# Softmax row sums: from tile additions in SBUF to TensorE products with a column of ones, accumulated in PSUM beside the output

## The chip, the cores and the metric

The program runs on one core of one Trainium2 chip. The metric is the time of one execution on the device, in microseconds (us). A core has five engines that run their own instruction lists in order and wait for one another through semaphores: TensorE (PE, matrix products, written to PSUM), VectorE (DVE), ScalarE (ACT), GpSimd (POOL) and SyncE (SP), which here issues the transfers. "PEld" in the profile is TensorE loading the stationary operand of a product.

## The reference

The program computes an attention with a cluster mask and then a mixture of experts. The change is in the attention alone: for each of 4 x 8 heads, 768 queries and 768 keys of 64 numbers.

```python
mask = q_assign[:, :, :, None] == k_assign[:, :, None, :]      # 16 clusters, by argmax
scores = np.where(mask, scale * np.matmul(q, k.transpose(0, 1, 3, 2)), -1e9)
attn = np.exp(scores - np.max(scores, axis=-1, keepdims=True))
attn = attn / (np.sum(attn, axis=-1, keepdims=True) + 1e-09)    # the row sum
attn_out = np.matmul(attn, v)
# then: gates by softmax over all logits, 8 rounds of normalisation, 8 experts
# out += P[:, e:e+1] * (np.maximum(x @ w1[e], 0.0) @ w2[e])
```

The row sum is over keys. It is needed once for each query and head, and the kernel divides by it after the product with v.

## The kernel before, in words

**Layout.** Two heads make a pair; there are 16 pairs. The 768 queries and keys are cut into six tiles of 128 (NT = 6). Weights are held transposed: a tile `pe` has 128 keys on the partitions and queries in the free dimension. So a sum over keys is a sum over the partitions of six tiles.

**Chunks.** A head's weights come in nine chunks (`CHUNKS`). For each u of three there is key tile 2u against queries 0 to 511, key tile 2u+1 against queries 0 to 511, and both key tiles against queries 512 to 767. Each chunk is 512 columns wide.

**Stages of a pair.** The loaded q and k are transposed on PE (L557), copied, and split into a high and a low part (L571 to L575, where the low part is a subtraction on DVE or POOL). Each position is assigned to a cluster (`assign_pair`, L593 to L635). `max_chunk` (L697, L701) takes the largest score of every query on PE and DVE. `max_rows` (L714 to L733) turns these into rows of the operand by way of DVE, ACT, POOL and PE. `exp_chunk` forms the scores again (L765, L766) into one of two PSUM tiles, and ACT writes their exponentials to `pe` (L772); 14 such tiles exist (`PB`).

**Sums before.** At the end of `exp_chunk` the six key tiles of a head are added element by element in SBUF into a tile `psum` (L791), each addition on POOL or on DVE. `norm` then sums over the partitions: a product with ones (L861), a copy (L868), three transposes (L872), the addition of 1e-9 and of flags for rows with nothing to attend to (L875), and a reciprocal (L886). The result is cut into three bf16 pieces (L890, L893), transposed (L897), spread over the rows of both heads (L908), and multiplied into `xT` (L913).

**Output.** `values` runs once for a pair. For each u it waits until the six chunks of both heads exist, and issues eight products with v into `av` (L824; the heads take columns 0 to 63 and 64 to 127 of the array). After the third u comes a small correcting product (L832), and ACT copies `av` to `xT` (L844). There is one `av` in PSUM.

**What sets the order.** A planner in the program places the steps on the engines ahead of time. Each step has a key (urgency), a cost that is written in the code, and sometimes a choice of engines with a reluctance. The planned order of each engine is then fixed. After the attention come the gates and the experts, whose instructions are written out by hand; their first weights are prepared within the last stretch of the attention (L1127, L1128, L1143, L1144).

Of the kernel before, what the change touches and what calls it, by code (L numbers as in the profile page):

```python
# [8 lines left out]
F32 = mybir.dt.float32  # L9
# [5 lines left out]
ALU = mybir.AluOpType  # L15
# [4 lines left out]
BIG = float(2.0**100)  # L20
P = 128
# [135 lines left out]
def attn_moe_kernel(  # L157
# [11 lines left out]
    nc = tc.nc  # L169
# [10 lines left out]
    NA, NB = 3, 4  # L180
    PB = 14
    N0 = 512
# [26 lines left out]
    Q = 32  # L209
# [102 lines left out]
    with ExitStack() as actx:  # L312
# [10 lines left out]
        def misc_tile():  # L323
            return ps_x.tile([P, 512], F32, name="misc_ps")
# [73 lines left out]
        for x in range(2):  # L398
# [8 lines left out]
        nc.vector.tensor_tensor(out=three12, in0=three12, in1=ident[0 : 3 * R, 2 * R : 3 * R], op=ALU.add)  # L407
        spread = sm.tile([3 * R, NT, 2, D], BF16, name="spread", bufs=1)
        nc.vector.tensor_copy(
            spread, three12.rearrange("r (x i) -> r i x", x=2).unsqueeze(3).broadcast_to([3 * R, NT, 2, D])  # L410
        )

        free = iter([(last[nm, i], f"{nm}{i}") for nm, i in kept])
# [9 lines left out]
        COSTS = [0.66, 0.46, 0.432, 0.214, 0.42]  # L423
        RELUCT = [0.05, 0.05, 0.5, 0.1, 0.2, 0.05, 0, 0, 0.3]

# [41 lines left out]
        t_nat, t_sc, t_pe, t_nh, t_vn = Tokens(2), Tokens(1), Tokens(PB), Tokens(6), Tokens(2)  # L467
        t_sum = Tokens(4)

# [17 lines left out]
        def load_group(n):  # L487
# [15 lines left out]
            for i in range(1, NT):  # L503
                e = yield (POOL, 0.687, RELUCT[3]), (DVE, 0.33)
                if i == 1:
                    vsum = nat.tile([P, G, D], F32, name="vsum", bufs=1)
                (nc.gpsimd if e == POOL else nc.vector).tensor_tensor(  # L507
                    out=vsum, in0=vn[:, :, 0, :] if i == 1 else vsum, in1=vn[:, :, i, :], op=ALU.add
                )
# [68 lines left out]
        def assign_pair(p):  # L578
# [128 lines left out]
        def max_rows(n):  # L707
# [12 lines left out]
            if n >= 8:  # L720
                yield ev["norm", n // 2 - 4]
            yield POOL, 0.1
            o = n % 2 * NT
            nc.gpsimd.tensor_scalar(out=flags[n // 2 % 4][:, o : o + NT], in0=mr, scalar1=-BIG / 2, scalar2=None, op0=ALU.is_le)
            yield t_x
# [22 lines left out]
        def exp_chunk(n, c):  # L748
# [26 lines left out]

            if c == 0:
                yield t_sum
                t["sum"] = work.tile([P, S], F32, name="psum", bufs=4)
                t["add"] = {}
            st, old = t["sum"], t["add"]  # L780
            if ni == 1:
                parts = [pe[:, 0]]
            else:
                parts = [pe[:, 0], pe[:, 1]]
            for part in parts:
                if a not in old:
                    old[a] = part
                    continue
                n_ = z - a
                e = yield (POOL, 0.33 + n_ * 0.0019), (DVE, 0.1 + n_ * 0.00125, RELUCT[2])  # L790
                (nc.gpsimd if e == POOL else nc.vector).tensor_tensor(out=st[:, a:z], in0=old[a], in1=part, op=ALU.add)  # L791
                old[a] = st[:, a:z]
            ev["s", n, c].set(plan)

        def release(p, c):

            c2 = c + 1 if c == 0 else c
            for x in range(2):
                yield ev["s", 2 * p + x, c2]
                t_pe.put(plan)  # L800

        def values(p):
# [10 lines left out]
            for u in range(NCH // 3):  # L813
# [36 lines left out]
        def norm(p):  # L850

            n = 2 * p
            b, h = divmod(n, H)
            for x in range(2):
                yield ev["s", n + x, NCH - 1]
            yield t_x
            yield PE, 0.75, 0.107, 0.64
            HS = S // 2
            ps = misc_tile()
            for g in range(4):  # L860
                nc.tensor.matmul(  # L861
                    ps[g * Q : (g + 1) * Q, 0:HS], ones[:, 0:Q], heads[n + g // 2]["sum"][:, g % 2 * HS : (g % 2 + 1) * HS], start=True, stop=True
                )
            for x in range(2):
                t_sum.put(plan)
            yield ACT, 0.48
            sc = work.tile([P, HS], F32, name="sc")
            nc.scalar.copy(sc, ps[:, 0:HS])  # L868
            yield PE, 0.36, 0.107, 0.1
            ps2 = misc_tile()  # L870
            for j in range(NT // 2):
                nc.tensor.transpose(out=ps2[:, j * P : (j + 1) * P], in_=sc[:, j * P : (j + 1) * P], identity=ident)  # L872
            yield DVE, 0.2
            rs = work.tile([P, R], F32, name="rs")
            nc.vector.scalar_tensor_tensor(  # L875
                out=rs.rearrange("p (g j) -> p g j", g=4),
                in0=ps2[:, 0 : NT // 2 * P].rearrange("p (j g q) -> p g j q", g=4, q=Q)[:, :, :, 0],
                scalar=1e-9,
                in1=flags[p % 4].rearrange("p (g j) -> p g j", g=4),
                op0=ALU.add,  # L880
# [546 lines left out]
```

## Time and profile before

| what | value |
|---|---|
| median of 3 runs | 2445.54 us (2442.27 to 2445.68) |
| the profiled execution, from its first to its last instruction | 2448.7 us, 3.2 above that median |
| mean granted TensorE clock | 0.984 |
| PE, DVE, ACT, POOL busy | 97%, 55%, 34%, 27% of the span |
| end of the attention's last output product | about 519 us |
| first product of the experts (L1219) starts | 532.4 us |
| L791, additions of weight tiles | 270 on POOL, 50 on DVE |

A group of instructions in the profile shows the line, the engine, the tiles written and read, the shapes (partitions x elements), the count, the busy time and mean duration, and the idle time of the engine just before them. A PE instruction's busy time includes its tail in the array, which overlaps with the next one's start. What a product holds the array for is therefore read from the distance of the starts, as the chain of waits lists it. A product of 32-bit floats appears as two instructions, and the page counts both; instruction lists of the program count it once. PEclk is the granted clock as a share of full speed.

### The profile page before, as it was taken

To read this page: it belongs to the slowest core of one execution; us is meant where nothing else is said; L and a number is where in the kernel's file an instruction comes from. 1 tells how busy PE (TensorE), PEld (TensorE's weight loads), DVE (VectorE), ACT (ScalarE), POOL (GpSimd) and SP (SyncE) were. 2 spreads that over 40 slices of the span, in tenths; PEclk is the share of its full clock that TensorE was granted. 3 is DMA by queue.
4 is the path that set the end of the run, shared out by engine and by line. 5 is a ranking of instruction groups with operands and counts; after the bars stand their busy time and mean duration, and the time that the engine had idled before them with its cause. 6 is when DMAs were issued, how large, how long until landed. Compare 5 with 4: busy or idle time off the path is not lost.

```text
span 2448.7 us, 32683 instructions
## 1 busy us (share of the span) xinstructions
PE 2383.3 (97%) x12848; PEld 1275.6 (52%) x12848; DVE 1342.4 (55%) x2354; ACT 836.1 (34%) x1616; POOL 672.4 (27%) x712
## 2 busy tenths in 40 slices
PE   7999999978999999999999999999999999999999
PEld 4555556534545555555555554555555555555554
DVE  7888888867655454545454445544444434444444
ACT  4555566544343333333333322212122121222211
POOL 5776777654153322223333201000000000000000
PEclk7999999989999999999999999999999999999999
DMA  6545465334466353535443334232222322223222
GB/s 145 119 101 121 102 150 152 84 125 155 164 220 218 146 196 133 212 142 186 171 156 129 127 135 145 95 113 99 95 95 96 111 102 95 95 95 109 104 104 90
DMA packets 154681, 320.29 MB, mean 131 GB/s; under 512 B 61088, under 2 KB 90528, under 8 KB 154016
## 3 DMA queue, kind: packets, MB, share of 16 engines
q1 hardware_dynamic: 154528, 318.21, 39.4%
q8 instruction: 101, 1.65, 0.3%
q14 instruction: 52, 0.43, 0.1%
HBM read 230.74 MB, written 58.72 MB: 118 GB/s over the span
## 4 chain that ended last, share of the span: by engine, by line
PE 86%; DVE 7%; issue 3%; ACT 2%; DMA 1%; POOL 0%; SPq 0%; POOLq 0%; ACTq 0%; DVEq 0%
PE h_ps L1219 34%; PE o_ps L1289 13%; PE o_ps L1287 13%; PE o_ps L1288 13%; PE av_ps L824 4%; PE max_ps L697 3%; PE exp_ps L765 2%; DVE mrt L701 2%; PE exp_ps L766 2%; DVE vsum L507 1%; PE misc_ps L557 1%; DVE hl L1235 1%; PE misc_ps L861 0%; ACT pe L772 0%; PE misc_ps L940 0%
## 5 line engine op out<-in xcount | busy, mean ns | idle before, releaser
L1219 PEld LDWEIGHTS <-wa 128*128 128x128 f16 x5376 | 528.1, 98 | 451.7 <-issue 26.9
L1219 PE MATMUL h_ps<-xsT,wa 128*128 128x384 f16 x3072 | 585.1, 327 | 9.2 <-DVE csum L1055 7.8
L1289 PE MATMUL o_ps<-wb,hl 128*128 128x512 f16 x1536 | 583.2, 380 | 1.4 <-DVE hl L1235 1.4
L1232 ACT ACTIVATE hh<-c 128x384 f16<-128x384 f32 x512 | 267.5, 523 | 927.7 <-DVE c L1247 916.6
L1288 PE MATMUL o_ps<-wb,hh 128*128 128x512 f16 x1536 | 583.1, 380 | 0.0
L1287 PE MATMUL o_ps<-wb,hh 128*128 128x512 f16 x1536 | 583.0, 380 | 0.0
L1235 DVE SCALAR_TENSOR_TENSOR hl<-c,hh 128x384 f16<-128x384 f32 x512 | 291.0, 568 | 493.1 <-ACT hh L1232 492.6
L1219 PE MATMUL h_ps<-xsB,wa 128*128 128x384 f16 x2304 | 421.4, 328 | 7.4 <-DVE c L1247 7.4
L1247 DVE SCALAR_TENSOR_TENSOR c<-h_ps,u 128x384 f32<-128x384 f32 x256 | 142.2, 555 | 193.1 <-PE h_ps L1219 193.0
L1289 PEld LDWEIGHTS <-hl 128*128 128x128 f16 x1536 | 150.5, 98 | 184.6 <-DVE hl L1235 3.4
L1247 DVE SCALAR_TENSOR_TENSOR u<-h_ps,m 128x384 f32<-128x384 f32 x256 | 142.3, 556 | 182.6 <-PE h_ps L1219 182.5
L791 POOL TENSOR_TENSOR psum<-psum,pe 128x512 f32<-128x512 f32 (+1 forms) x207 | 227.2, 1115 | 54.2 <-ACT pe L772 46.6
L1287 PEld LDWEIGHTS <-hh 128*128 128x128 f16 x1536 | 151.0, 98 | 139.2 <-issue 0.6
L1288 PEld LDWEIGHTS <-hh 128*128 128x128 f16 x1536 | 150.4, 98 | 139.6 <-issue 0.6
L701 DVE TENSOR_REDUCE mrt<-max_ps 128x1 f32<-128x512 f32 (+1 forms) x288 | 190.5, 683 | 46.3 <-PE max_ps L697 44.6
L1252 ACT ACTIVATE c<-h_ps 128x384 f32<-128x384 f32 x128 | 62.7, 490 | 424.7 <-PE h_ps L1219 424.7
L772 ACT ACTIVATE pe<-exp_ps 128x512 f32<-128x512 f32 x288 | 166.5, 597 | 88.8 <-PE exp_ps L766 82.6
L1101 POOL TENSOR_TENSOR r<-r 128x256 f32<-128x256 f32 x124 | 88.3, 733 | 372.4 <-ACT r L1092 370.0
L1307 DVE SCALAR_TENSOR_TENSOR acc<-o_ps,gates,acc 128x512 f32<-128x512 f32 x168 | 125.4, 747 | 41.3 <-PE o_ps L1289 41.1
L824 PE MATMUL av_ps<-pe,vn 128*64 128x512 f32 (+1 forms) x768 | 138.5, 504 | 0.0
L697 PE MATMUL max_ps<-kX,qX 96*128 96x256 f32 (+1 forms) x384 | 126.9, 393 | 5.5 <-DVE mrt L701 2.6
L766 PE MATMUL exp_ps<-qX,kX 98*128 98x512 f32 (+1 forms) x384 | 128.5, 347 | 0.0
(200 smaller groups left out, 1920.8 us busy)
## 6 DMA issues: line engine op xcount, KB each, us to landing
wa<-wd SPq DMA_DIRECT2D x96, 896.0 KB
wb<-wd SPq DMA_DIRECT2D x96, 512.0 KB
r<-in_moe_w SPq DMA_DIRECT2D x64, 512.0 KB
wd<-wa SPq DMA_DIRECT2D x32, 896.0 KB
scan<-in_moe_w SPq DMA_DIRECT2D x56, 512.0 KB
wd<-wb SPq DMA_DIRECT2D x32, 512.0 KB
qn<-in_q SPq DMA_DIRECT2D x16, 384.0 KB
kn<-in_k SPq DMA_DIRECT2D x16, 384.0 KB
```

The costliest lines, as they stand in the source:

```text
L697: nc.tensor.matmul(ps[:, y * (z - a) : (y + 1) * (z - a)], t["qa"][0:96, i * P : (i + 1) * P], t["k2"][0:96, a:z], start=True, stop=True)
L701: nc.vector.tensor_reduce(out=t["mr"][:, i0 : i0 + ni, ni - 1], in_=ps.rearrange("p (x c) -> p x c", x=ni), axis=AX, op=ALU.max)
L766: nc.tensor.matmul(o, t["k2"][0:98, ki], t["qa"][0:98, a:z], start=False, stop=True)
L791: (nc.gpsimd if e == POOL else nc.vector).tensor_tensor(out=st[:, a:z], in0=old[a], in1=part, op=ALU.add)
L824: nc.tensor.matmul(av[o, a:z], vn[:, i, :], heads[t]["pe", c][:, i - i0], start=(i == 0), stop=False, skip_group_check=True)
L1219: nc.tensor.matmul(ps[:, 0:HB], wa[:, w_, a, c, :], x[:, x_, c, :], start=(first and s_ == 0), stop=(s_ == len(steps) - 1), skip_group_che ...
L1232: nc.scalar.activation(hh[:, 2 - i, o], src, AF.Relu)
L1235: nc.vector.scalar_tensor_tensor(out=hl[:, 2 - i, o], in0=src, scalar=0.0, in1=hh[:, 2 - i, o], op0=ALU.max, op1=ALU.subtract)
L1247: nc.vector.scalar_tensor_tensor(out=t, in0=ps[:, 0:HB], scalar=KAPPA, in1=x, op0=ALU.mult, op1=ALU.add)
L1287: nc.tensor.matmul(po[i], hh[:, t, ti], wbh[:, t], start=(first and t == 0), stop=False)
L1288: nc.tensor.matmul(po[i], hh[:, t, ti], wbl[:, t], start=False, stop=False)
L1289: nc.tensor.matmul(po[i], hl[:, t, ti], wbh[:, t], start=False, stop=(last and t == 1))
```

## The change

The additions at the end of `exp_chunk` go, and with them the tiles `psum` and the process `release` that freed a weight tile once it was added and used. In their place, `values` issues after its eight output products of each u another 24: stationary is `pick`, 128 x 32, all zero but for a column of ones, moving are 128 queries of a weight tile, and the result goes to columns 768 to 895 of `av`, in the same bank of PSUM as the last 256 output columns. A block of 32 rows there belongs to one of four column blocks of the array. `piece` says which: query tiles 0 to 3 go to blocks 0 to 3, with one row for each head, and tiles 4 and 5 of both heads share the four blocks in a third row. So row sums accumulate over all key tiles in PSUM. After the last u ACT copies the 128 columns (`sc`), one transpose replaces three, and the rest of `norm` is as before, with `flags` and `spread` in the new order.

With it come: 20 weight tiles (`PB`), all six of a u given back after its 24 products; flags written by two POOL instructions and not one; and other reluctances, by which the planner gives the value sums (`vsum`), a product of the assignment (`ix`) and the low parts (`qL`, `kL`) to POOL where it can.

```diff
-    PB = 14
+    PB = 20
...
+        QG = P // Q
+        assert NT == QG + 2
...
+        pick = sm.tile([P, 3, Q], F32, name="pick", bufs=1)
+        nc.vector.memset(pick, 0.0)
+        for s_ in range(3):
+            nc.vector.memset(pick[:, s_, s_ : s_ + 1], 1.0)
+
+        def piece(x, i):
+            return (i, x) if i < QG else (2 * x + i - QG, 2)
...
-        RELUCT = [0.05, 0.05, 0.5, 0.1, 0.2, 0.05, 0, 0, 0.3]
+        RELUCT = [0.05, 0.05, 0.5, 0.1, 0.2, 0.05, 0.5, 0, 0.3]
...
-                e = yield (POOL, 0.687, RELUCT[3]), (DVE, 0.33)
+                e = yield (POOL, 0.687), (DVE, 0.33, RELUCT[2])
...
-            e = yield (DVE, 0.469), (POOL, 0.86, RELUCT[8])
+            e = yield (DVE, 0.469, RELUCT[8]), (POOL, 0.86)
...
-            for part in parts:
-                if a not in old:
-                    old[a] = part
-                    continue
-                n_ = z - a
-                e = yield (POOL, 0.33 + n_ * 0.0019), (DVE, 0.1 + n_ * 0.00125, RELUCT[2])
-                (nc.gpsimd if e == POOL else nc.vector).tensor_tensor(out=st[:, a:z], in0=old[a], in1=part, op=ALU.add)
-                old[a] = st[:, a:z]
-            ev["s", n, c].set(plan)
...
-                    plan.spawn(release(p, c), plan.now.key)
+                yield PE, 1.32, 0.107, 0.1
+                for k_ in (2 * u, 2 * u + 1):
+                    for i0, i1 in ((0, QG), (QG, NT)):
+                        for x in range(2):
+                            c = 3 * u + (k_ % 2 if i0 == 0 else 2)
+                            pe = heads[n + x]["pe", c][:, k_ - CHUNKS[c][0]]
+                            for i in range(i0, i1):
+                                g, s_ = piece(x, i)
+                                nc.tensor.matmul(
+                                    av[g * Q : (g + 1) * Q, S : S + P],
+                                    pick[:, s_],
+                                    pe[:, (i - i0) * P : (i - i0 + 1) * P],
+                                    start=False,
+                                    stop=(k_ == NT - 1 and s_ == 2),
+                                    skip_group_check=True,
+                                )
+                for _ in range(6):
+                    t_pe.put(plan)
+            yield ACT, 0.3
+            sc = heads[n]["sc"] = work.tile([P, P], F32, name="sc")
+            nc.scalar.copy(sc, av[:, S : S + P])
+            ev["sums", p].set(plan)
...
-            yield PE, 0.75, 0.107, 0.64
-            HS = S // 2
-            ps = misc_tile()
-            for g in range(4):
-                nc.tensor.matmul(
-                    ps[g * Q : (g + 1) * Q, 0:HS], ones[:, 0:Q], heads[n + g // 2]["sum"][:, g % 2 * HS : (g % 2 + 1) * HS], start=True, stop=True
-                )
...
-            for j in range(NT // 2):
-                nc.tensor.transpose(out=ps2[:, j * P : (j + 1) * P], in_=sc[:, j * P : (j + 1) * P], identity=ident)
+            nc.tensor.transpose(out=ps2[:, 0:P], in_=heads[n]["sc"], identity=ident)
```

Line numbers shift: the eight output products are at L824 before and L811 after, the 24 new ones at L822, the correcting product at L832 and L840, the copy of the sums at L868 and L834.

Three places show how instructions move. The first is PE at the end of the second pair's third u, with what each row waits for. Before:

```order
L697 MATMUL max_ps<-kX_156,qX_153 128x512 [waits DVE_49]
L824 MATMUL av_ps<-pe,vn 64x512 x4
L824 MATMUL av_ps<-pe,vn 64x256 [waits Activation_49] x2
L824 MATMUL av_ps<-pe,vn 64x256 x2
L832 MATMUL av_ps<-nht_207,ve 128x512 [waits DMAHW6_49]
L832 MATMUL av_ps<-nht_207,ve 128x256
L697 MATMUL max_ps<-kX_156,qX_153 128x256 [waits DVE_49]
```

And now:

```order
L811 MATMUL av_ps<-pe,vn 64x512 x4
L811 MATMUL av_ps<-pe,vn 64x256
L811 MATMUL av_ps<-pe,vn 64x256 [waits Activation_49]
L811 MATMUL av_ps<-pe,vn 64x256 x2
L822 MATMUL av_ps<-pe,pick 32x128 x24
L708 MATMUL max_ps<-kX_174,qX_170 128x512 [waits DMAHW3_49,DMAHW5_49,DMAHW2_49,DVE_49]
L777 MATMUL exp_ps<-qL_161,kH_165 128x512 [waits PE_49]
L778 MATMUL exp_ps<-qX_169,kX_173 128x512 [waits DMAHW5_49,DMAHW4_49]
L708 MATMUL max_ps<-kX_174,qX_170 128x512 [waits DVE_49]
L840 MATMUL av_ps<-nht_207,ve 128x512 [waits Activation_49]
L840 MATMUL av_ps<-nht_207,ve 128x256
```

The 24 new products stand behind the eight, four products of other stages lie between them and the correcting product, and that one now waits for ACT, whose copy of the sums reads the same tile.

The second place is POOL at about the third pair, where `mm` and `flags` are the row maxima's pieces. Before:

```order
L791 TENSOR_TENSOR psum<-psum,pe 128x256 x2
L791 TENSOR_TENSOR psum<-psum,pe 128x512
L791 TENSOR_TENSOR psum<-psum,pe 128x256
L791 TENSOR_TENSOR psum<-psum,pe 128x512 x2
L791 TENSOR_TENSOR psum<-psum,pe 128x256 x2
L575 TENSOR_TENSOR qL_160<-qn,qH_149 128x512
L575 TENSOR_TENSOR kL_152<-kn,kH_164 128x512
```

And now:

```order
L887 TENSOR_TENSOR rs<-rs,rr 128x12 x2
L729 TENSOR_SCALAR mm_201<-mr_1162 128x6
L730 TENSOR_TENSOR mm_201<-mr_1162,mm_201 128x6
L736 TENSOR_SCALAR flags_218<-mr_1162 128x4
L736 TENSOR_SCALAR flags_218<-mr_1162 128x2
L586 TENSOR_TENSOR qL_159<-qn,qH_148 128x512
L586 TENSOR_TENSOR kL_151<-kn,kH_163 128x512
```

No addition of weights is left on POOL; the small steps of the row maxima follow one another directly.

The third is PE at the very end of the attention. Before:

```order
L824 MATMUL av_ps<-pe,vn 64x512 x4
L824 MATMUL av_ps<-pe,vn 64x256 x4
L832 MATMUL av_ps<-nht_206,ve 128x512
L832 MATMUL av_ps<-nht_206,ve 128x256
L861 MATMUL misc_ps<-psum,ones 32x384 x4
L872 MATMUL misc_ps<-ident,sc 128x128 x3
```

And now:

```order
L811 MATMUL av_ps<-pe,vn 64x512 x4
L811 MATMUL av_ps<-pe,vn 64x256 x4
L822 MATMUL av_ps<-pe,pick 32x128 x24
L840 MATMUL av_ps<-nht_206,ve 128x512
L840 MATMUL av_ps<-nht_206,ve 128x256
L866 MATMUL misc_ps<-ident,sc 128x128
```

The 24 stand ahead of the correcting product, and the product with ones and two transposes are gone. Over the whole attention PE has 1152 products at L822, 64 fewer at L861 and 32 fewer transposes of `sc`.

More of the change, by code (lines that the diff above doesn't have):

```diff
@@ L408, in attn_moe_kernel @@
         spread = sm.tile([3 * R, NT, 2, D], BF16, name="spread", bufs=1)
+        QG = P // Q
+        assert NT == QG + 2
         nc.vector.tensor_copy(
-            spread, three12.rearrange("r (x i) -> r i x", x=2).unsqueeze(3).broadcast_to([3 * R, NT, 2, D])
+            spread[:, 0:QG], three12[:, 0 : 2 * QG].rearrange("r (x i) -> r i x", x=2).unsqueeze(3).broadcast_to([3 * R, QG, 2, D])
         )
+        nc.vector.tensor_copy(
+            spread[:, QG:NT], three12[:, 2 * QG : R].rearrange("r (x i) -> r i x", x=2).unsqueeze(3).broadcast_to([3 * R, 2, 2, D])
+        )
[5 more added lines that the diff above has]
+            return (i, x) if i < QG else (2 * x + i - QG, 2)
         free = iter([(last[nm, i], f"{nm}{i}") for nm, i in kept])
@@ L467, in attn_moe_kernel @@
         t_nat, t_sc, t_pe, t_nh, t_vn = Tokens(2), Tokens(1), Tokens(PB), Tokens(6), Tokens(2)
-        t_sum = Tokens(4)
         pairs = {}
@@ L721, in max_rows @@
                 yield ev["norm", n // 2 - 4]
-            yield POOL, 0.1
-            o = n % 2 * NT
-            nc.gpsimd.tensor_scalar(out=flags[n // 2 % 4][:, o : o + NT], in0=mr, scalar1=-BIG / 2, scalar2=None, op0=ALU.is_le)
+            yield POOL, 0.2
+            x = n % 2
+            for to, src in ((slice(x * QG, (x + 1) * QG), mr[:, 0:QG]), (slice(2 * QG + 2 * x, 2 * QG + 2 * x + 2), mr[:, QG:NT])):
+                nc.gpsimd.tensor_scalar(out=flags[n // 2 % 4][:, to], in0=src, scalar1=-BIG / 2, scalar2=None, op0=ALU.is_le)
             yield t_x
@@ L774, in exp_chunk @@
             ev["p", n, c].set(plan)
[L776 to L784, printed above, removed]
-            for part in parts:
-                if a not in old:
-                    old[a] = part
-                    continue
-                n_ = z - a
-                e = yield (POOL, 0.33 + n_ * 0.0019), (DVE, 0.1 + n_ * 0.00125, RELUCT[2])
-                (nc.gpsimd if e == POOL else nc.vector).tensor_tensor(out=st[:, a:z], in0=old[a], in1=part, op=ALU.add)
-                old[a] = st[:, a:z]
-            ev["s", n, c].set(plan)
[L795 to L800, printed above, removed]
         def values(p):
@@ L826, in values @@
                             )
-                    plan.spawn(release(p, c), plan.now.key)
+                yield PE, 1.32, 0.107, 0.1
[13 more added lines that the diff above has]
+                                    skip_group_check=True,
+                                )
+                for _ in range(6):
[4 more added lines that the diff above has]
+            ev["sums", p].set(plan)
             for x in range(2):
@@ L853, in norm @@
             b, h = divmod(n, H)
-            for x in range(2):
-                yield ev["s", n + x, NCH - 1]
+            yield ev["sums", p]
             yield t_x
-            yield PE, 0.75, 0.107, 0.64
-            HS = S // 2
-            ps = misc_tile()
-            for g in range(4):
-                nc.tensor.matmul(
-                    ps[g * Q : (g + 1) * Q, 0:HS], ones[:, 0:Q], heads[n + g // 2]["sum"][:, g % 2 * HS : (g % 2 + 1) * HS], start=True, stop=True
-                )
[L864 to L869, printed above, removed]
+            yield PE, 0.16, 0.107, 0.1
             ps2 = misc_tile()
-            for j in range(NT // 2):
-                nc.tensor.transpose(out=ps2[:, j * P : (j + 1) * P], in_=sc[:, j * P : (j + 1) * P], identity=ident)
+            nc.tensor.transpose(out=ps2[:, 0:P], in_=heads[n]["sc"], identity=ident)
             yield DVE, 0.2
@@ L875, in norm @@
             nc.vector.scalar_tensor_tensor(
-                out=rs.rearrange("p (g j) -> p g j", g=4),
-                in0=ps2[:, 0 : NT // 2 * P].rearrange("p (j g q) -> p g j q", g=4, q=Q)[:, :, :, 0],
+                out=rs.rearrange("p (s g) -> p s g", g=QG),
+                in0=ps2[:, 0:P].rearrange("p (g q) -> p q g", g=QG)[:, 0:3],
                 scalar=1e-9,
-                in1=flags[p % 4].rearrange("p (g j) -> p g j", g=4),
+                in1=flags[p % 4].rearrange("p (s g) -> p s g", g=QG),
                 op0=ALU.add,
```

## The prediction

> **What bounds the kernel now.** I read the page first, then busy times by stretch, then the chain of waits and the waits of the stretch that the change touches.
>
> ```profile
> span 2448.7 us, 32683 instructions
> PE 2383.3 (97%) x12848; PEld 1275.6 (52%) x12848; DVE 1342.4 (55%) x2354; ACT 836.1 (34%) x1616; POOL 672.4 (27%) x712
> ...
> PE   7999999978999999999999999999999999999999
> DVE  7888888867655454545454445544444434444444
> POOL 5776777654153322223333201000000000000000
> ```
>
> The average of 27% for POOL hides the attention: in the first eight of 40 slices POOL and DVE are both at 0.7 to 0.8, and PE is at 0.9 or more. The stretches say it in microseconds (columns: PE, PEld, DVE, ACT, POOL busy, granted clock, transfers):
>
> ```profile
> 0.00:60.00 60.00, 43.25 (x171) 26.62 (x173) 46.58 (x113) 24.72 (x50) 33.19 (x51) 0.74 0.66 143
> 60.00:519.00 459.00, 445.17 (x2605) 262.34 (x2601) 384.20 (x625) 263.78 (x583) 335.49 (x400) 0.98 0.48 111
> 519.00:536.00 17.00, 10.44 (x58) 4.75 (x57) 7.71 (x21) 4.33 (x12) 0.42 (x2) 0.65 0.78 286
> 536.00:600.00 64.00, 49.67 (x236) 24.96 (x236) 48.09 (x88) 27.33 (x43) 37.11 (x28) 0.88 0.35 127
> ```
>
> From 60 to 519 us the attention runs at its steady pace. PE is idle for 459.0 - 445.2 = 13.8 us, DVE for 75, POOL for 124. So PE is the fullest engine, and the change gives it work. How full it truly is, the waits tell. The first row is PE's own, the rest are those of its weight loads, whose idle time begins earlier, since a product's tail no longer covers it:
>
> ```profile
> PE misc_ps L728 <- POOL mm L719: 3.3, 2, 1.6
> ...
> PEld exp_ps L765 <- ACT pe L772: 13.3, 29, 0.8
> PEld max_ps L697 <- DVE mrt L701: 10.4, 25, 1.2
> PEld L628 <- DVE om L619: 6.0, 7, 1.8
> PEld misc_ps L728 <- POOL mm L719: 4.5, 3, 2.1
> PEld misc_ps L861 <- POOL psum L791: 2.3, 7, 0.4
> PEld misc_ps L728 <- POOL psum L791: 1.8, 4, 0.6
> PEld max_ps L697 <- DVE mr L714: 1.7, 3, 0.6
> ```
>
> These seven come to 40.0 us, of which DVE and POOL end 26.7 and ACT 13.3. The time in which PE truly stands still lies between 13.8 (nothing of its tail left) and 40.0; I take the middle, 27. The clock of 0.98 costs another 2% of 459, about 9. The rest, 423 of 459 us, is work that PE must do. All that the change can win in this stretch is those 36 us.
>
> **What is added on PE.** The trace has no product of 32 columns on 128 moving ones. The nearest is the product with ones, L861: the same four column blocks, 384 columns, two instructions each. The chain of waits lists it between its neighbours (start, us, what):
>
> ```profile
> 288.25 0.24 PE max_ps L697
> 288.49 0.78 PE misc_ps L861 x8
> 289.27 0.43 PE max_ps L697
> ...
> 290.91 0.34 PE misc_ps L872 x3
> ```
>
> Four products of 384 columns, one in each block, take 0.78 us: the blocks run together. And the next full-width product takes 0.43 where the one before the blocks takes 0.24, so the return to the full array costs 0.19. One u has 24 products of 128 columns, which is six rounds of four, so 6 x 128 = 768 columns, twice those of L861: 2 x 0.78 = 1.56 us, with the entry into the blocks counted twice. If the entry costs what the return does, and none is paid, it is 2 x (0.78 - 0.19) = 1.18. With one entry it would be 1.37; I take 1.45, nearer the upper end, because a weight load has only a third of L861's columns to hide behind. For 48 times that is 69.6. Counted in the planned order, PE changes between blocks and full width 216 times and not 186, so there are 15 returns more: 15 x 0.19 = 2.9. Removed are 16 x 0.78 = 12.5 for L861, and two of three transposes at L872, 16 x 0.23 = 3.6. **PE gains 69.6 + 2.9 - 12.5 - 3.6 = 56 us**, between 40 (at 1.18, no more returns) and 62 (at 1.56).
>
> **What is taken from POOL and DVE.**
>
> ```profile
> L791 POOL TENSOR_TENSOR psum<-psum,pe 128x512 f32<-128x512 f32 (+1 forms) x200 | 219.7, 1116 | 52.1 <-ACT pe L772 45.9 <-DVE mrt L701 1.7 <-ACT rr L890 1.2
> L791 POOL TENSOR_TENSOR psum<-pe 128x512 f32<-128x512 f32 (+1 forms) x59 | 60.2, 1029 | 35.3 <-ACT pe L772 34.4
> L791 DVE TENSOR_TENSOR psum<-psum,pe 128x256 f32<-128x256 f32 (+1 forms) x48 | 50.0, 1057 | 11.1 <-ACT pe L772 6.0 <-POOL psum L791 4.4 <-ACT rr L890 0.5
> L507 DVE TENSOR_TENSOR vsum<-vsum,vn x25: 405/534/1507, 64.2 to 421.0; 128x256 f32<-128x256 f32 x25
> L507 POOL TENSOR_TENSOR vsum<-vsum,vn x3: 730/980/1107, 61.2 to 63.4; 128x256 f32<-128x256 f32 x3
> ```
>
> POOL loses 219.7 + 60.2 = 280 of its 335 us, DVE 50 of 384. The fourth row suggests that POOL's adding also slows DVE: the same addition takes DVE 405 ns at best and up to 1507 (least, median, most). (The Trainium skill, SBUF — State Buffer, "Who interferes with whom", says that a DVE instruction with two inputs in SBUF contends with POOL's reads; the spread agrees.) The moved work (34 value sums, 8 products of the assignment, some 36 low parts) costs POOL about 1 us each by the median of the last row, 80 in all, hidden because it then has 135 of some 490 us to do. It lies early in a pair, whose loads come two pairs ahead; without that cover the low parts would come about a microsecond later for a pair, 16 in all. Flags in two instructions add 32 small ones there. DVE is left with roughly 300 of 490.
>
> So the 26.7 us of waits for DVE and POOL lose most of their cause. Those for ACT keep it, but PE then has 1.45 us of work at a time that needs nothing new from ACT. I let 22 of the 27 us go. Of the clock's 9 us I give back half, 4.5, since fewer pauses should leave fewer slow stretches:
>
> ```profile
> 240.00:248.00 8.00, 8.00 (x31) 3.52 (x31) 4.89 (x6) 3.73 (x8) 5.66 (x6) 0.57 0.27 58
> ```
>
> Here the clock was halved for most of 8 us, and nowhere before it did PE wait longer than the 1.6 us of the row at L728 above. (The Trainium skill, TensorE: Matmul & The Clock Gate, "What's actually happening", lets an idle window of some 3.4 us slow the clock. By that rule a PE without pauses would get all 9 us back, and the sum would be 4.5 lower. This stretch, with PE busy for all of its 8 us, does not bear the rule out.)
>
> **A new wait.** The correcting product L840 now waits for ACT's copy of the sums. Behind it stand all later products of PE. Between the 24 products and it are four others, 0.24 each, so about 0.95 us. ACT's copy is a third of the old one, which stands below the exponential that may be ahead of it:
>
> ```profile
> L772 ACT ACTIVATE pe<-exp_ps 128x512 f32<-128x512 f32 x275 | 158.8, 597 | 84.4 <-PE exp_ps L766 78.4 <-POOL psum L791 1.4 <-POOL rs L893 0.5
> ...
> 520.06 0.48 ACT L868 COPY sc<-misc_ps 128x384 f32<-128x384 f32 x1
> ```
>
> Even at the old 0.48, behind one exponential of 0.6 it comes after 1.1 us: 0.15 late, 16 times, 2 us. Without the cover it would be 17.
>
> **The end of the attention.** Nothing of PE's slack hides here:
>
> ```profile
> 518.08 2.75 DVE wa L1128 x4
> ...
> 518.35 1.04 ACT L1143 CAST wb<-r 128x1024 f16<-128x1024 f32 x1
> ...
> 520.84 1.14 DVE wb L1144
> 521.97 0.09 DVE rs L875
> ```
>
> DVE prepares weights after its last addition, and the last sums wait behind that until 521.97. Without additions DVE can begin as soon as ACT has cast, but the last cast binds until 519.39, and the 24 products add 1.45 before the sums. I count 1 us won; late next is still L1144.
>
> **The sum**: 56 - 22 - 4.5 + 2 - 1 = +31 us (30.5), so 2448.7 + 31 = 2479.7 for a profiled execution. That lies 3.2 above the median of the runs, so the forecast for these is 2445.5 + 30.5 = **2476 us**. PE would then do 423 + 56 = 479 us of work in about 490: nearly nothing else is left to win there. What comes after 600 us is not touched.
>
> **Rivals.**
>
> *Faster, by the start and the hand-over* (chance 0.12). In 60 to 519 us even a full gain gives 56 - 27 - 9 = +20: the trace leaves no room for a faster steady pace. But from 0 to 60 and from 519 to 600 us PE is idle for 16.8 + 6.6 + 14.3 = 37.7 us and the clock loses 0.26 x 60 + 0.35 x 17 + 0.12 x 64 = 29. If a POOL and DVE without additions bring the first pairs and the first expert weights forward, part of this goes. It decides from 20 us on, over half of the idle time there; at 33 won the time is 2445.5 + 20 - 33 = 2433. Against it: the start waits for loads and the end is a chain of small dependent steps.
>
> *No change* (0.10): the same with about 20 won, 2446.
>
> *PE bound by issuing instructions* (0.08). A group is 24 products, each a load and a product in two instructions: 96. The densest stretch of small ones that I find is this:
>
> ```profile
> 122.36 0.18 PE misc_ps L628 x3
> ```
>
> That is 0.06 us for a load and a product, 30 ns for an instruction. If that is the pace of issuing and not of the 128 columns, a group takes 96 x 0.03 = 2.9 us, and 48 of them 70 us more than I count: 2546. Against it: L861's 16 instructions fit into 0.78, 49 ns each, which leaves it open, but its four blocks start together. (The Trainium skill, TensorE: Matmul & The Clock Gate, "Wait — 56ns, not 53.3ns?", gives a floor of about 25 ns between starts of products. For 48 products that is an estimate of 1.2 us, under my price; only if loads count as well does it come to 2.4.)
>
> *New waits eat the gain* (0.12): L840's copy stands behind two exponentials, 16 us instead of 2, so 2490.
>
> That the change does not do what it says is excluded by the order: no addition is left, 1152 products have come.
>
> **How the numbers follow.** The forecast's case has 0.58; its own range is 2451 to 2497 (40 with 27 and 9 won gives +5; 62 with 12 won and nothing of the clock gives +51). With the rivals above it, slower has 0.58 + 0.12 + 0.08 = 0.78. What can be told from no change here is about 0.2%, 5 us: same has 0.10, faster 0.12. The range of 2443 to 2505 leaves out the faster case and the issue-bound one, 0.2 together.
>
> **What would show it.** Right: the 24 products of a u start over 1.3 to 1.6 us; POOL's busy time in the attention falls by about 200 us; waits for DVE and POOL on PE's loads shrink to a few us; PE's idle time in the steady stretch is a few us while that stretch grows by some 30; after it all is as long as before. Wrong: groups far from 1.45 us (each 0.1 us is 4.8 on the sum), PE's waits as large as before (then it is nearer 2495), or an attention that starts or ends much earlier relative to its steady part.

## The result, and the profile after

The changed kernel takes **2490.2 us** (median of 4 runs, 2488.6 to 2493.2), the kernel before 2445.6 (median of 4, 2442.3 to 2446.1): a ratio of 1.0184, 95% interval 1.017 to 1.0198. So it is slower by 44.6 us. The forecast was 2476, with a range of 2443 to 2505.

The page of the changed kernel, its span, busy times and the POOL row of the 40 slices:

```profile
span 2487.1 us, 36542 instructions
PE 2424.1 (97%) x14992; PEld 1327.0 (53%) x14992; DVE 1241.4 (50%) x2247; ACT 826.1 (33%) x1600; POOL 452.8 (18%) x552
...
POOL 5222222204144222333232221000000000000000
```

POOL has lost 220 us of work (672.4 before) and DVE 101 (1342.4 before). In most slices of the attention, the first nine, POOL is at two tenths where it was at five to seven. Yet the kernel is slower.

Busy times by stretch after the change (PE, PEld, DVE, ACT, POOL, granted clock, transfers):

```profile
0.00:60.00 60.00, 40.20 (x150) 24.87 (x150) 44.83 (x104) 21.12 (x42) 30.61 (x52) 0.69 0.61 139
60.00:519.00 459.00, 452.37 (x4329) 292.39 (x4333) 275.51 (x512) 237.64 (x534) 117.22 (x232) 1.00 0.49 112
519.00:561.00 42.00, 40.39 (x455) 24.49 (x454) 11.56 (x20) 20.53 (x44) 1.29 (x6) 1.00 0.04 13
```

In 60 to 519 us PE now idles 6.6 us where it idled 13.8, and its clock is full where it was 0.98. POOL does 117 us of work there and not 335. The attention, however, goes on until 561 us.

Where the time went is read from the correcting product, which ends each pair's output, and from the first expert product. Both rows of the lines of the tiles `av_ps` and `h_ps`, first of the kernel before, then of the changed one (shortest, median and longest in ns, then the first and last start in us):

```profile
L832 PE MATMUL av_ps<-nht,ve x32: 269/383/501, 77.3 to 518.9; 4*128 4x512 f32 x16, 4*128 4x256 f32 x16
...
L1219 PE MATMUL h_ps<-xsB,wa x2304: 322/326/528, 532.4 to 2436.2; 128*128 128x384 f16 x192
```

```profile
L840 PE MATMUL av_ps<-nht,ve x32: 269/385/499, 84.3 to 560.6; 4*128 4x512 f32 x16, 4*128 4x256 f32 x16
...
L1213 PE MATMUL h_ps<-xsB,wa x2304: 322/326/528, 571.6 to 2474.6; 128*128 128x384 f16 x192
```

| part | before | after | difference |
|---|---|---|---|
| start to the first pair's output | 77.3 | 84.3 | +7.0 |
| from there to the last pair's output (steady) | 441.6 | 476.3 | +34.7 |
| hand-over to the first expert product | 13.5 | 11.0 | -2.5 |
| experts to the end of the span | 1916.3 | 1915.5 | -0.8 |
| span | 2448.7 | 2487.1 | +38.4 |

The spans differ by 38.4 us and the medians by 44.6. The time of a run is some 2 us more than its span (2489.3 for this profiled execution of the changed kernel), so the profiled execution of before lay about 5 us above its median, and that of the change 1 below.

The added products, in the chain of waits of the changed kernel (start, us, what), at three places of the attention:

```profile
65.19 1.45 PE av_ps L822 x48
...
306.03 1.45 PE av_ps L822 x48
...
453.92 1.45 PE av_ps L822 x48
```

The price of a group is the 1.45 us of the prediction; of the 40 groups that the chain lists between 60 and 519 us, 38 have it and two have 1.31. And what PE itself, then its weight loads, waited for in 60 to 519 us (us in total, times, longest):

```profile
PE exp_ps L777 <- ACT pe L784: 3.2, 10, 1.1
PE max_ps L708 <- DVE mrt L712: 1.5, 4, 0.6
...
PEld exp_ps L777 <- ACT pe L784: 9.7, 18, 1.6
...
PEld max_ps L708 <- DVE mrt L712: 5.3, 14, 1.0
PEld av_ps L840 <- issue: 4.8, 13, 0.4
```

The waits for POOL and for the assignment on DVE are nearly gone from the list of weight loads, as forecast: 1.6 and 0.3 us are left. They took much less time with them than their sum of microseconds.

### The profile page after: what moved, and what is told of

The parts are those of the page before. It is cut to its first block, busy times and chain, and to the rows that moved or that the text cites. A ratio compares the mean times of both kernels' runs of the same rounds, so it can differ in the third digit from the quotient of the medians.

```text
span 2487.1 us, 36542 instructions
## 1 busy us (share of the span) xinstructions
PE 2424.1 (97%) x14992; PEld 1327.0 (53%) x14992; DVE 1241.4 (50%) x2247; ACT 826.1 (33%) x1600; POOL 452.8 (18%) x552
## 4 chain that ended last, share of the span: by engine, by line
PE 89%; DVE 4%; issue 4%; ACT 2%; DMA 1%; POOL 1%; SPq 0%; POOLq 0%; ACTq 0%; DVEq 0%
PE h_ps L1213 33%; PE o_ps L1283 12%; PE o_ps L1281 12%; PE o_ps L1282 12%; PE av_ps L811 5%; PE max_ps L708 3%; PE exp_ps L777 3%; PE av_ps L822 3%; PE exp_ps L778 2%; PE misc_ps L568 1%; DVE hl L1229 1%; DVE mrt L712 1%; ACT pe L784 0%; PE misc_ps L604 0%; DVE c L1241 0%
## 5 line engine op out<-in xcount | busy, mean ns | idle before, releaser
L811 PE MATMUL av_ps<-pe,vn 128*64 128x512 f32 (+1 forms) x768 | 134.4, 492 | 0.0
L708 PE MATMUL max_ps<-kX,qX 96*128 96x256 f32 (+1 forms) x384 | 125.3, 392 | 8.4 <-DMA qX<-ot 4.2
L1109 POOL TENSOR_TENSOR wb<-r,wb 128x1024 f16<-128x1024 f32 x31 | 66.9, 2159 | 188.5 <-ACT wb L1108 188.5
```

Source lines behind the costliest of these rows:

```text
L708: nc.tensor.matmul(ps[:, y * (z - a) : (y + 1) * (z - a)], t["qa"][0:96, i * P : (i + 1) * P], t["k2"][0:96, a:z], start=True, stop=True)
L811: nc.tensor.matmul(av[o, a:z], vn[:, i, :], heads[t]["pe", c][:, i - i0], start=(i == 0), stop=False, skip_group_check=True)
```

## The experiments

Each ran beside the kernel before on the same chip, and the ratios are to that. "First maximum" is the start of the first product L697 (L708 after), "first" and "last output" the first and last start of the correcting product, in the profiled execution.

| kernel | median us | ratio (95%) | first maximum | first output | last output |
|---|---|---|---|---|---|
| before | 2445.0 to 2448.4 | 1 | 23.4 | 77.3 | 518.9 |
| the change | 2490.2 | 1.0184 (1.017 to 1.0198) | 29.0 | 84.3 | 560.6 |
| add only | 2509.5 | 1.0255 (1.0231 to 1.0279) | 23.9 | 80.7 | 578.1 |
| half the products | 2454.4 | 1.003 (1.0018 to 1.0043) | 29.0 | 81.6 | 526.8 |
| relief only, new reluctances | 2433.0 | 0.9936 (0.9917 to 0.9956) | 29.1 | 80.3 | 504.7 |
| relief only, old reluctances | 2420.7 | 0.9891 (0.9874 to 0.9907) | 23.6 | 74.7 | 494.1 |
| new reluctances alone | 2452.7 | 1.0027 (1.0016 to 1.0038) | 28.9 | 81.5 | 518.2 |
| the change, old reluctances | 2482.7 | 1.0151 (1.0137 to 1.0165) | 23.7 | 77.9 | 554.8 |
| the change, first value sums on DVE | 2488.0 | 1.0171 (1.0154 to 1.0188) | 26.6 | 81.3 | 558.9 |
| the change, old reluctance for low parts | 2487.5 | 1.0163 (1.0148 to 1.0178) | 23.2 | 80.2 | 558.8 |
| the change, joined | 2483.4 | 1.0147 (1.0127 to 1.0168) | 29.1 | 83.3 | 556.4 |
| joined, old reluctances | 2484.7 | 1.0157 (1.0138 to 1.0177) | 24.3 | 78.8 | 562.3 |
| before, with the change's last step | 2438.5 | 0.9975 (0.9963 to 0.9986) | 23.7 | 76.1 | 506.8 |

### Half of the added products

```diff
-                yield PE, 1.32, 0.107, 0.1
-                for k_ in (2 * u, 2 * u + 1):
+                yield PE, 0.66, 0.107, 0.1
+                for k_ in (2 * u,):
```

> The changed kernel with only one of the two key tiles of a u summed: 12 products with the column of ones in a group and not 24 (half of each row sum is left out, so the output is another). If the time is PE's work, by the columns of these products: 48 x 0.72 = 35 us less than the changed kernel, a little of it given back since PE is then less full (up to 4 us of clock): 2455 to 2460 us. If a group costs by its entry, its exit and the place where it interrupts the other work, and not by its columns: 2475 us or more.

2454.4 us, 35.8 under the change. A group in its chain of waits:

```profile
64.72 0.79 PE av_ps L822 x24
```

So 12 products cost 0.66 us less than 24, and 48 x 0.66 = 32 of the 36 us; where the other 4 lie is not shown, and the time is 0.6 us under the first theory's range. The time goes by the number of these products. What a group costs beside that is 1.45 - 2 x 0.66 = 0.13 us. The second theory falls. (Fewer products also means fewer columns and fewer instructions; which of the two it is, the last experiment tells.)

### The added products without the relief

```diff
+                yield PE, 1.32, 0.107, 0.1
+                for k_ in (2 * u, 2 * u + 1):
+                    for i0, i1 in ((0, QG), (QG, NT)):
...
+                                nc.tensor.matmul(
+                                    av[g * Q : (g + 1) * Q, S : S + P],
...
                     plan.spawn(release(p, c), plan.now.key)
```

> The kernel before with all its additions and its own row sums, plus the 24 products of each u (their result is not used): the added work without the relief. By PE's work: 48 x 1.45 = 69.6, and 77 more changes between blocks and full width in the planned order at 0.15 = 11.5, less the clock's 8.5 and some 6 of waits that a fuller PE covers: 2446 + 67 = about 2512 us (2500 to 2522). If the additions' waits were worth the 22 us of the prediction, the distance to the changed kernel is 16 + 6 + 22 = 44 and not some 22: 2534 us.

2509.5 us, 64 above before. The middle stretch of this kernel:

```profile
60.00:519.00 459.00, 450.79 (x4375) 287.13 (x4372) 345.10 (x597) 230.92 (x508) 290.14 (x352) 1.00 0.48 112
```

All additions are there and DVE and POOL are as busy for each pair as before (345 and 290 us in this stretch). Still PE idles 459.0 - 450.8 = 8.2 us, not 13.8. By these two executions 5.6 of the 7.2 us of idle time that the change recovered come from the added work itself, which fills PE's pauses, and 1.6 are left for the relief of DVE and POOL. But the kernels with the relief and all the added products idle 5.9 to 10.3 us in the same stretch (5.9 the change with old reluctances, 10.3 the joined one with them), so 1.6 cannot be told from nothing.

The times say it better. By PE's work alone this kernel should stand 22 us above the changed one, and by the prediction's waits 44 (2534 us). It stands 19 above it, and 27 above the changed kernel with the old reluctances, which this kernel has too. By the ratios the 27 are 25. So if the 22 holds, the relief is worth 3 to 5 us beside the added work, and the second theory falls.

### The relief without the added products

Four products of one key tile stand in for the 72 of a pair, so that the later steps have a value to work on:

```diff
-                yield PE, 1.32, 0.107, 0.1
-                for k_ in (2 * u, 2 * u + 1):
...
+                if u == NCH // 3 - 1:
+                    yield PE, 0.25, 0.107, 0.1
+                    for g in range(QG):
+                        nc.tensor.matmul(
+                            av[g * Q : (g + 1) * Q, S : S + P],
+                            ones[:, 0:Q],
+                            heads[n]["pe", 3 * u][:, 0, g * P : (g + 1) * P],
```

> The changed kernel without nearly all of the added products: the additions on POOL and DVE are gone, the reluctances are the new ones, but PE gets only four small products for a pair (the row sums are then of one key tile alone). It measures what the relief of POOL and DVE is worth by itself. PE's work is some 11 us less than in the kernel before (12.5 and 3.6 removed, 16 groups of about 0.3 added). By the prediction's terms (22 us of waits and 4.5 of the clock come back): 2446 - 11 - 22 - 4.5 = 2408 us. If only about 6 us of waits come back, with all of the clock's 8.5 and 5 us lost at the start: 2446 - 11 - 6 - 8.5 + 5 = 2425 us. If the relief is worth nothing, or the moved work costs as much: 2435 us or more.

2433.0 us: 12.8 less than before by the medians (15.7 by the ratio), hardly more than the 11 of PE work that left, and above both expectations that give the relief a value. But the moved work is in this kernel as well, so it was run a second time with the reluctances of before:

```diff
-        RELUCT = [0.05, 0.05, 0.5, 0.1, 0.2, 0.05, 0.5, 0, 0.3]
+        RELUCT = [0.05, 0.05, 0.5, 0.1, 0.2, 0.05, 0, 0, 0.3]
...
-                e = yield (POOL, 0.687), (DVE, 0.33, RELUCT[2])
+                e = yield (POOL, 0.687, RELUCT[3]), (DVE, 0.33)
...
-            e = yield (DVE, 0.469, RELUCT[8]), (POOL, 0.86)
+            e = yield (DVE, 0.469), (POOL, 0.86, RELUCT[8])
```

> The kernel with the additions gone and four small products for a pair in place of the 72, now with the old reluctances: the relief of POOL and DVE without the moved work (the row sums are again of one key tile alone). If the relief recovers nothing of PE's waits and the moved work costs 7.5 us as in the changed kernel: the 2433 us of the same kernel with the new reluctances, less 7.5, so 2423 to 2428 us, with PE's idle time between 60 and 500 us about as large as before. If the relief was worth the prediction's 22 us and the moved work in the steady stretch hid it: 2408 to 2414 us.

2420.7 us, 26.3 less than before, 2 below the first theory's range and 7 above the second's. 60 to 490 us, all of it attention in both, before and then in this kernel:

```profile
60.00:490.00 430.00, 417.83 (x2460) 247.87 (x2457) 365.24 (x606) 246.63 (x548) 313.62 (x380) 0.98 0.51 119
```

```profile
60.00:490.00 430.00, 420.44 (x2538) 255.03 (x2536) 286.04 (x546) 253.51 (x569) 83.45 (x197) 1.00 0.49 116
```

230 us less on POOL and 79 less on DVE leave PE idle for 9.6 us where it was 12.2. What relief is worth to PE's pauses is 2.6 us of 430. Some 11 of the 26 us are PE work that left; the clock of 1.00 for 0.98 is up to 8.6 us of this pair of executions; 2.6 came at the start and 3.2 at the hand-over to the experts (10.3 us for 13.5). The spans of this pair differ by 29.6 us, so these parts belong to the spans and not to the medians; how much of the clock's part the relief brought is not shown.

### The reluctances

On the kernel before, the new reluctances alone (the diff above, read from below):

> The kernel before, additions and all, with the new reluctances alone: value sums, a product of the assignment and 60 of 76 low parts on POOL. If this moved work is what brings the first pair's output 3 us later in the changed kernel and in the one without the products: 2446 + 3, less 16 planned changes between blocks and full width at 0.15 = 2.4: 2446 us, with the first pair's last product at about 80.5 and not at 77.8. And since POOL is then fuller than before (some 400 of 459 us), waits for POOL would show if these were what costs PE: 2455 us or more. If the moved work is nothing: 2443 us, first pair at 77.8.

2452.7 us, 7.6 above before on the same chip, and the first maximum at 28.9 us. Its middle stretch:

```profile
60.00:519.00 459.00, 444.77 (x2642) 262.83 (x2642) 374.58 (x619) 261.50 (x575) 361.01 (x438) 1.00 0.49 114
```

PE idles 14.2 us there, as before (13.8), although POOL has 26 us more to do: no new waits of PE in this stretch. And its clock is 1.00 with all the additions and as many pauses, one of them of 2.8 us. So neither the additions nor the pauses as such explain the 0.98 of the kernel before. The first output comes at 81.5 us, 4.2 later than before, where 80.5 was expected. The 2446 us are missed by 6.6; where the rest of the 7.6 us lies is not shown, since the profiled spans differ by only 2.4. On the changed kernel, the old ones:

> The changed kernel with the old reluctances: value sums and the assignment's product back on DVE, 36 of 76 low parts on DVE. If the moved work costs 3 us at the start and nothing later: 2490 - 3 = 2487 us, first pair's last product at about 82 and not 84.8. If DVE's relief is what PE needs (DVE is then some 30 us fuller in the attention): 2492 us or more.

2482.7 us, 7.5 under the change, and the first maximum at 23.7. The moved work costs 7 to 8 us in either kernel, and 12 in the one that has neither the additions nor most of the added products (2433.0 for 2420.7). A large part of it lies at the start: with the moved work the first output comes 4.2, 6.4 and 5.6 us later in these three pairs of kernels. The chain of waits of before, up to the first maximum, and then of the change:

```profile
18.04 0.38 DVE halves L402 x3
...
21.43 1.99 DMA qX<-ot
23.43 0.78 PE max_ps L697
```

```profile
19.75 3.66 DVE halves L402 x4
...
24.38 0.68 ACT ot L646
25.07 0.41 ACT kH L582
25.48 0.07 issue
25.55 0.73 POOL kL L586
...
26.98 1.99 DMA qX<-ot
28.98 0.78 PE max_ps L708
```

Four copies of 4 x 64 numbers take 3.7 us. They begin 1.7 us later than before and take 3.3 us longer, and the transfer to `qX` begins 5.6 us later. POOL's timeline of the changed kernel shows what runs beside them:

```profile
18.79 0.76 POOL L518 TENSOR_TENSOR vsum<-vsum,vn 128x256 f32<-128x256 f32 x1
19.52 1.25 POOL L586 TENSOR_TENSOR qL<-qn,qH 128x512 fp32r<-128x512 f32 x1
20.74 0.71 POOL L518 TENSOR_TENSOR vsum<-vsum,vn 128x256 f32<-128x256 f32 x1
21.42 1.26 POOL L586 TENSOR_TENSOR kL<-kn,kH 128x512 fp32r<-128x512 f32 x1
22.64 0.71 POOL L586 TENSOR_TENSOR qL<-qn,qH 128x256 fp32r<-128x256 f32 x1
```

POOL adds and subtracts without a pause from 18.8 to 23.4 us, and DVE's copies end when it does. PE meanwhile waits for the last value sum:

```profile
PE misc_ps L524 <- POOL vsum L518: 4.8, 1, 4.8
```

Two kernels ask which part of the moved work it is. The first puts only the value sums of the first group back on DVE:

```diff
-                e = yield (POOL, 0.687), (DVE, 0.33, RELUCT[2])
+                e = yield (POOL, 0.687, 5.0 if n == 0 else 0), (DVE, 0.33, 0 if n == 0 else RELUCT[2])
```

> The changed kernel with one thing put back: the value sums of the first group, in the first 25 us, are on DVE again; all other moved work stays on POOL. If these sums, one behind the other on POOL, are what delays the start (the product that sums them came at 21.5 and not 16.7 us, and DVE's small copies ran at 0.95 us each and not 0.18 beside them): first maximum product at 23.5 to 25 us and not 29.0, time 2490 - 5 = 2484 to 2486 us. If the low parts on POOL delay it: 29 us, 2489 us or more.

The second only the low parts:

```diff
-        RELUCT = [0.05, 0.05, 0.5, 0.1, 0.2, 0.05, 0.5, 0, 0.3]
+        RELUCT = [0.05, 0.05, 0.5, 0.1, 0.2, 0.05, 0, 0, 0.3]
```

> The changed kernel with the old reluctance for the low parts alone: 37 of 76 on DVE (2 in the changed kernel), value sums still on POOL. If the value sums delay the start: first maximum product still at about 28 to 29 us, 2488 us or more. If the low parts do: 23.5 to 25 us, 2484 to 2486 us.

The rows of `max_ps` and `halves`, of the first kernel and then of the second (first and last start behind the durations):

```profile
L708 PE MATMUL max_ps<-kX,qX x384: 276/392/796, 26.6 to 523.7; 96*128 96x512 f32 x96, 96*128 96x256 f32 x96
...
L402 DVE COPY halves<-of x4: 175/175/602, 20.2 to 20.9; 4x64 f32<-4x64 f32 x4
```

```profile
L708 PE MATMUL max_ps<-kX,qX x384: 277/392/797, 23.2 to 527.8; 96*128 96x512 f32 x96, 96*128 96x256 f32 x96
...
L402 DVE COPY halves<-of x4: 172/176/176, 20.3 to 20.6; 4x64 f32<-4x64 f32 x4
```

Either one frees DVE's copies, all but one of 602 ns in the first. The first kernel brings the first maximum forward by 2.4 us and the second by 5.8, as far as both together do (23.7 with the old reluctances). So for the first maximum it is enough to put back the low parts, of which one stands right ahead of the first transfer to the operand `qX`. But the times of 2484 to 2486 us that either expectation gives for this case did not come: the first output is at 81.3 and 80.2 us, and at 77.9 only with both put back. In time the two cannot be told from each other (2488.0 and 2487.5, with overlapping intervals), nor surely from the change itself.

### The groups behind the output products

```diff
-                yield PE, 2.8, 0.107, 0.43
+                yield PE, 4.12, 0.107, 0.43
...
-                yield PE, 1.32, 0.107, 0.1
                 for k_ in (2 * u, 2 * u + 1):
```

> The changed kernel with the 24 products directly behind the eight output products of the same u, as one step of the planner. Same products, 37 changes between blocks and full width fewer in the planned order. If such a change costs PE 0.15 to 0.19 us: 5.5 to 7 us less than the changed kernel, 2483 to 2485 us. If the place of the groups among the other steps matters more (a step of 4.1 us holds up the products that feed the exponentials): 2492 us or more.

2483.4 us, 6.8 under the change by the medians and 9.0 by the ratios: 37 changes of width fewer, so 0.18 to 0.24 us for each if all of it is theirs. The row at L697 had 0.19. With the old reluctances as well:

> The changed kernel with both repairs: the 24 products directly behind the eight, and the old reluctances. If start and changes of width are separate costs, both gains add: 2483.4 - 7.5 = 2476 us (2474 to 2478). If they are the same time seen twice (PE waits where it does not change): 2482 us or more.

2484.7 us (2481.2 to 2491.5), on a chip where before took 2448.4. The two gains do not add: by ratio it is not better than either alone. Its first maximum is early (24.3), but from first to last output it took 483.5 us where the change took 476.3, in an execution that was the slowest of its four. Why the steady part lost what the start won stays open.

### The last step of the change alone

The additions stay in SBUF as before, with the old reluctances. Of the change only the end is kept: 12 products of 128 columns from the two added tiles in place of four of 384, a copy of 128 columns in place of 384, one transpose in place of three, flags and `spread` in the new order.

```diff
-            for g in range(4):
-                nc.tensor.matmul(
-                    ps[g * Q : (g + 1) * Q, 0:HS], ones[:, 0:Q], heads[n + g // 2]["sum"][:, g % 2 * HS : (g % 2 + 1) * HS], start=True, stop=True
-                )
+            for i0, i1 in ((0, QG), (QG, NT)):
+                for x in range(2):
+                    for i in range(i0, i1):
+                        g, s_ = piece(x, i)
+                        nc.tensor.matmul(
+                            ps[g * Q : (g + 1) * Q, 0:P], pick[:, s_], heads[n + x]["sum"][:, i * P : (i + 1) * P], start=(s_ == 0), stop=(s_ == 2)
+                        )
...
-            for j in range(NT // 2):
-                nc.tensor.transpose(out=ps2[:, j * P : (j + 1) * P], in_=sc[:, j * P : (j + 1) * P], identity=ident)
+            nc.tensor.transpose(out=ps2[:, 0:P], in_=sc, identity=ident)
```

> The kernel before, with its additions in SBUF and the old reluctances, and only the end of the row sums as in the change: 12 products of 128 columns with the column of ones in place of four of 384 (0.73 for 0.78 us), one transpose for three, a copy of 128 columns for one of 384, flags in two instructions. PE's work is 0.23 + 0.05 us less for each of 16 pairs, 4.5 us, and the planned order has 14 changes between blocks and full width fewer, 2.1 us. If PE's work is the time: 2446 - 6.6 = 2439 us (2437 to 2442). If it lies in PE's waits: 2445 us or more.

2438.5 us, ratio 0.9975 (0.9963 to 0.9986): 6.5 us faster than before, and faster than either kernel. The 12 products, in its chain of waits, cost what the four did (0.78):

```profile
105.16 0.79 PE misc_ps L876 x24
```

Both are 1536 columns, and the 12 are three times as many instructions. So the price of these products goes by their columns and not by their number of instructions.

What is won is thus the two transposes (16 x 0.23 = 3.7) and 14 changes of width (2.1 to 2.6): 5.8 to 6.3 us of PE work, and 6.5 us of time.

## Why the prediction was right, and where it was not

**PE is the bound: right.** Four kernels move PE's work by a known amount, and the time follows: 36 us for 30 to 35 expected (half the products), 64 for 67 (add only), 6.8 for 5.5 to 7 (joined), 6.5 for 6.6 (the last step). In the change DVE and POOL lost 320 us of busy time, and the time went up. (In the first eight slices POOL's row reads five to seven tenths, and not the seven to eight that the prediction gives for both engines.)

**PE gains 56 us: right in its main term.** A group takes 1.45 us, so 48 x 1.45 stands. In the steady part 45 groups are 65.3 us; less 15 x (0.78 + 0.23) = 15.2 removed, less 7.2 of idle time and 0.02 x 459 = 9.2 of clock, that gives 33.7, and 34.7 was measured. The 2.9 us of 15 more returns are not seen apart.

**22 of 27 us of waits come back: wrong, and this is the term that was mis-sized.** The prediction put the time in which PE stands still between 13.8 and 40.0 us and took the middle. The lower end was near the truth: the waits in the list of weight loads mostly lay beside products that were still running, so only PE's own idle time of 13.8 us could be won. Of that 7.2 came back, most of it (5.6, add only) because PE had more to do, and not because DVE and POOL had less; the relief alone recovers 2.6 of 430 us, and by the times it is worth 3 to 5 beside the added work. So 22 should have been about 7, which is 15 us.

**Half of the clock's 9 us: its reason is not borne out.** The clock went from 0.98 to 1.00 in 60 to 519 us, so in the profiled pair all 9 came back. But the kernel with the new reluctances alone has 1.00 there too, with all the additions, 14.2 us of idle time and a pause of 2.8 us. So neither the relief nor fewer pauses are needed for it, and part of the 9 may belong to the one execution of before that was profiled, which lay 5 us above its median. Why that execution had slow stretches stays open. (By the rule of the Trainium skill, TensorE: Matmul & The Clock Gate, "What's actually happening", a PE without pauses would keep its full clock; the rows after the change agree with it, from 60 to 561 us at 1.00. The slow stretch of before at 240 us, with a pause of 1.6 us ahead of it, it still does not explain.) The prediction's "nowhere before it" holds from 60 us on; in the first 60 us PE had waited up to 4.6.

**The moved work at nothing: wrong.** The prediction hid 80 us of moved work behind an idle POOL. In the steady part that holds (476.3 us with it, 554.8 - 77.9 = 476.9 without). At the start POOL is not idle in the sense that matters: the first pair's low parts stand behind the value sums in its queue, and the first maximum comes 5.6 us later. The runs give 7.5 us for it in this kernel, of which 6.4 are there at the first output. The prediction had named a microsecond "for a pair" as the price without cover and looked for the cover in averages over 490 us; the first pair has no earlier pair to hide behind.

**The new wait at L840, 2 us: not there.** L840's loads wait 4.8 us for "issue", as L832's did before (5.3), and ACT holds this product up for less than 1 us in all. **The end, -1:** it was -2.5.

By the prediction's own terms, corrected: 56 - 7 - 9 + 0 - 2.5 + 7.5 = 45 us, against the 44.6 of the medians. That the two agree is luck, because 7, 9 and 2.5 are read from the profiled pair, whose spans differ by 38.4. In that pair 56 is too much by some 6: the 2.9 for returns is not seen, and the first pair's three groups (4.4 us, less 1.0 removed) fall into the start, whose +7.0 already holds them. Against the medians the clock's term may be smaller than 9; by how much is not known. The errors went both ways (+15 and +7.5 for waits and moved work, -4.5, -2 and -1.5 for clock, L840 and the end), and so the forecast of +30.5 missed by only 14.

**The rivals.** *Faster by the start and the hand-over* named the right places with the wrong sign at one: the hand-over gave 2.5, the start cost 7. *PE bound by issuing* is excluded: 48 instructions of products and 48 of loads fit into 1.45 us, and half of them into 0.79. *New waits at L840* is excluded by the row above; that the time was the 2490 of that rival is an accident of other terms.

## What to carry to other kernels

Work that is moved to the engine that bounds the stretch costs its full price, and the relief of engines that do not bound it is worth at most the bound engine's own idle time and what it frees at the start and the end: read that from its busy row, not from the waits of its weight loads, which begin before its last product has ended. Here the fuller engine swallowed most of its small pauses by itself, so they were not a gain of the relief. And a move onto an engine that is idle on average must be looked at in the first microseconds, where nothing earlier covers it.

## What the hardware showed beside that

**DVE's small copies wait for POOL.** The four copies of `halves` take 172 to 176 ns each in the kernel before and 753 to 1296 (median 946) beside POOL's unbroken two-input work. The rows of before and of the change:

```profile
L402 DVE COPY halves<-of x4: 172/175/176, 17.9 to 18.2; 4x64 f32<-4x64 f32 x4
...
L402 DVE COPY halves<-of x4: 753/946/1296, 19.7 to 22.6; 4x64 f32<-4x64 f32 x4
```

The instructions of POOL at that time take 0.71 to 1.26 us, so each copy lasts about as long as one of them. In the kernel with the first value sums back on DVE only the first copy is long (602 ns): it ends with POOL's subtraction at 20.7 us, and the three behind it are short again. The Trainium skill, SBUF — State Buffer, "Who interferes with whom", has copies among the instructions of DVE that can take the port pair shared with GpSimd, and lets the later one block for the whole instruction of the other. The durations agree. That the block is the port was not tried by itself.

**A slow clock at the start costs little here.** In 0 to 60 us the granted clock was 0.69 in the profiled execution of the change and 1.00 in that of the joined kernel:

```profile
0.00:60.00 60.00, 41.33 (x151) 25.06 (x151) 44.46 (x105) 21.13 (x42) 30.63 (x52) 1.00 0.61 139
```

Yet their first maximum came at 29.0 and 29.1 us and their first output at 84.3 and 83.3. There PE waits for others, and its slower products fit into those waits. The prediction's rival counted 0.26 x 60 us of the clock as time to be won at the start; these two executions show about 1 us of it.
